# Four output tiles carried ahead of the last weights, and one even load of the first expert's w1

## The chip, the cores and the metric

The kernel runs on one core of a Trainium2 chip. The metric is the device time of one execution in microseconds (us).

## The reference, cut to what matters

```python
def _attn_ref(q, k, v):                       # (8, 8, 576, 64) each
    k_p = k.reshape(B, H, 72, 8, D).mean(axis=3)
    v_p = v.reshape(B, H, 72, 8, D).mean(axis=3)
    attn = softmax(scale * q @ k_p.T)         # 576 x 72 for each head
    return attn @ v_p
# x: the heads side by side, 4608 tokens x 512
def _moe_ref(x, phi, w1, w2):                 # 8 experts, 4 slots each, F = 1024
    logits = x @ phi                          # 4608 x 32
    d = softmax(logits, axis=0)               # over the tokens
    slot_input = (d.T @ x).reshape(8, 4, 512)
    for e in range(8):
        h = np.maximum(slot_input[e] @ w1[e], 0.0)
        slot_out[e] = h @ w2[e]
    c = softmax(logits, axis=1)               # over the 32 slots
    return c @ slot_out                       # 4608 x 512, float32
```

All inputs and the output are float32. w1 and w2 are 16 MB each in float32.

## The kernel before

**Loads.** All large loads are issued by GpSimd and cast to bfloat16 on the way. The order is written by hand: k, q and v of a pair of batches, then the next pair's, with w1 of the experts between them as soon as the second pair is in hand, then w2 behind the last v. `load_w1(0, 1, True)` (L105) sends the first expert's w1 in two column ranges. The first 2560 of the 4096 columns of a row go as rows 0 to 111, 112 to 119 and 120 to 127 (L110), the other 1536 columns of all rows follow in one transfer (L112). All other experts' w1 go in one transfer each time. The last part of w2 (expert 6 from its fourth block on, and expert 7) comes in two halves of 256 columns, each in four pieces (`PIECES`, L92; loads at L537). The very last piece of a half is one block, `J7`, of expert 7.

**Attention** takes the pairs of batches in turn: keys and values are pooled, scores, exponentials, and the products u (L338), from which also the logits come. It ends in `G`, the slot inputs, and `cT`, the transposed exponentials of the logits, in which each slot's weight for each token lies.

**First layer.** `hidden` (L559) and `turn_hidden` (L575) make `hT` for all experts. From here on the order of TensorE (PE), VectorE (DVE), ScalarE (ACT) and SyncE (SP) is the written one (`manual_schedule`, L550).

**Second layer.** `second_layer` (L583) adds into `so_ps`, one PSUM bank, with four groups of 32 partitions (g = fj % 4) that are added up later by the last product. The matmuls of the experts 0 to 3 run at once for all 512 columns; then come five `busy(512)` matmuls (L615), which compute nothing that is used, then experts 4 and 5, and the pieces of experts 6 and 7 as they land.

**Output.** A token tile n has 128 tokens; `GROUPS` (L57) joins 2, 2, 2, 4, 6, 8 and 12 tiles into areas of the output that are contiguous, `tokens(n)` picks a tile's columns of `cT`. `product` (L640) makes one tile in one of five PSUM banks, `put` scales its rows on ACT (engine 0) or DVE (engine 1), `store` (L636) issues the transfer on SP. Tiles 0 to 9 are made in two halves of columns, the first half while the second half's weights are loading; tiles 10 to 35 whole.

**Carrying.** In `begin(half)` (L662) the second layer's sum without `J7` is scaled to `so_a`. A carried tile gets `J7`'s share in another way: `zT` (L604 to L609) is `cT` times the hidden values of that block, so that zT times the piece of w2, plus tokens times `so_a`, is the finished tile before the last second-layer matmul has run. Before, tiles 0 and 1 are carried, tile 0 ahead of that last matmul and tile 1 behind it; `so`, the full sum, is scaled on DVE, and the tiles from 2 on use it. The stores of the first half are tile 0, 1, 2 and 3 one by one, then 4 and 5, 6 and 7, 8 and 9; those of the second half 0, 1, then 2 and 3, 4 and 5, 6 to 9; then three large ones of 1.5, 2 and 3 MB.

Of the kernel before, what the change touches and what calls it, by code (L numbers as in the profile page):

```python
# [8 lines left out]
FP = mybir.dt.float32  # L9
BF = mybir.dt.bfloat16  # L10
# [8 lines left out]
def kernel(  # L19
# [10 lines left out]
    nc = tc.nc  # L30
# [4 lines left out]
    DM = H * D  # L35
    E = moe_w1.shape[0]
    F = moe_w1.shape[2]
    NS = moe_phi.shape[1]
# [9 lines left out]
    DJ = DM // 128  # L48
    FJ = F // 128
# [23 lines left out]
    w1_sb = persist.tile([128, E, DJ, F], BF)  # L73
    cT = persist.tile([128, 2, B * S // 2], BF)
    hT = persist.tile([128, E, FJ, NS], BF)
# [14 lines left out]
    HC = DM // 2  # L90
    halves = [slice(0, HC), slice(HC, DM)]
# [4 lines left out]
    def load(src, pair):  # L96
        nonlocal loaded
        loaded += 1
        t = big[:, loaded % 4]
        nc.gpsimd.dma_start(out=t, in_=pair_of(src, pair))  # L100
        return t.rearrange("p (t d) -> p t d", d=D)

    UNEVEN = 2560

    def load_w1(e, n, uneven=False):  # L105
        dst = w1_sb[:, e:e + n].rearrange("p e j f -> p e (j f)")
        src = moe_w1[e:e + n].rearrange("e (p j) f -> p e (j f)", j=DJ)
        if uneven:
            for p0, p1 in ((0, 112), (112, 120), (120, 128)):
                nc.gpsimd.dma_start(out=dst[p0:p1, :, 0:UNEVEN], in_=src[p0:p1, :, 0:UNEVEN])  # L110
            dst, src = dst[:, :, UNEVEN:], src[:, :, UNEVEN:]
        nc.gpsimd.dma_start(out=dst, in_=src)  # L112

    w2_at = {}

# [55 lines left out]
    with tc.tile_pool(name="tmp", bufs=1) as tmp:  # L171
# [8 lines left out]
        for r in range(2):  # L180
            rows = slice(r * D, (r + 1) * D)
            nc.vector.tensor_copy(out=iphi[rows, :, r, 0:D],
                                  in_=ident[rows, rows].rearrange("p d -> p () d").to_broadcast([D, HQ, D]))
# [6 lines left out]
        for j in range(J):  # L190
            nc.tensor.matmul(out=phi_ps, lhsT=sel[:, j].rearrange("p r a j -> p (r a j)"), rhs=spread[:, j],  # L191
                             start=(j == 0), stop=(j == J - 1))
# [4 lines left out]
    hz = consts.tile([128, 128], BF)  # L197
# [13 lines left out]
    def after_k(p):  # L211
        if p + 1 < NP:
            q_sb[p + 1] = load(q, p + 1)
        if p == 1:
            load_w1(0, 1, True)

    def after_q(p):
        if p + 1 < NP:
            v_sb[p + 1] = load(v, p + 1)
        if p == 1:  # L220
            load_w1(1, 1)
        if p == 2:
            load_w1(2, 3)
            load_w1(5, 3)
# [35 lines left out]
    def prepare_kq(pair):  # L260

        means = kvpool.tile([128, NR, 2, D], BF, name="kmeans")
        yield from pool_stage(k_sb[pair], means, lambda: after_k(pair))
        kp[pair] = kvpool.tile([128, BH, SP], BF, name="kp", bufs=2)
        dst = kp[pair].rearrange("p n (r i) -> p r n i", r=NR)
        yield from turn_stage(means, lambda r0, r1, ps: nc.vector.tensor_copy(out=dst[:, r0:r1], in_=ps))
        for n, t0 in enumerate(range(0, NU, 6)):
            ps = ps_m.tile([128, 6, BH, NI], BF, name="q_ps", tag="m")
            for t in range(6):
                tt = 2 * (t0 + t)  # L270
                nc.tensor.transpose(out=ps[:, t].rearrange("p n i -> p (n i)"),  # L271
                                    in_=q_sb[pair][:, tt:tt + 2, :].rearrange("p t d -> p (t d)"), identity=ident)
            dst = qT[pair][:, :, t0:t0 + 6, :].rearrange("p n t i -> p t n i")
            if n % 3 == 1:
                nc.scalar.copy(out=dst, in_=ps)  # L275
            else:
                nc.vector.tensor_copy(out=dst, in_=ps)  # L277
            if n == NU // 6 - 1:
                after_q(pair)
            yield  # L280
# [133 lines left out]
    for g, (rows, base) in enumerate(GROUPS):  # L414
        cols = cT[:, :, base // 2:base // 2 + 64 * rows].rearrange("p r (i s) -> p s r i", s=rows // 2)
# [47 lines left out]
    def tokens(n):  # L463

        g, r = TILES[n]
        rows, base = GROUPS[g]
        step, c0 = rows // 2, base // 2 + r // 2
        return cT[:, r % 2, c0:c0 + 127 * step + 1:step]
# [63 lines left out]
    w2_half = {}  # L532
    for half, cols in enumerate(halves):
        for e, j0, j1 in PIECES:
# [3 lines left out]
                                in_=moe_w2[e].rearrange("(p j) d -> p j d", j=FJ)[:, j0:j1, cols])  # L538
# [12 lines left out]
    post = ctx.enter_context(tc.tile_pool(name="post", bufs=1))  # L551
    ps_o = ctx.enter_context(tc.tile_pool(name="ps_o", bufs=1, space=PSUM))
    ps_f = ctx.enter_context(tc.tile_pool(name="ps_f", bufs=5, space=PSUM))
# [26 lines left out]

    so_ps = ps_o.tile([128, DM], FP, name="so_ps")

    def second_layer(e, j0=0, j1=FJ, half=None):  # L583
        cols = slice(0, DM) if half is None else halves[half]
        for fj in range(j0, j1):
            g = fj % NG
            nc.tensor.matmul(out=so_ps[g * NS:(g + 1) * NS, cols], lhsT=hT[:, e, fj],  # L587
                             rhs=w2_at[e, fj] if half is None else w2_half[e, fj, half],
                             start=(e == 0 and fj < NG), stop=(e == E - 1 and fj >= NG), skip_group_check=True)

    hidden(0)
# [10 lines left out]
    J7 = FJ - 1  # L602
    P7 = (E - 1) % NG * NS
    nc.vector.tensor_scalar(out=hz[P7:P7 + NS], in0=h_sb[(E - 1) // NG][P7:P7 + NS, J7:F:FJ], scalar1=recC[P7:P7 + NS],  # L604
                            scalar2=None, op0=ALU.mult)
    z_ps = ps_f.tile([128, 2, 128], FP, name="z_ps", tag="f")
    nc.tensor.matmul(out=z_ps, lhsT=hz, rhs=cT[:, :, 0:128], start=True, stop=True)
    zT = post.tile([128, 2, 128], BF)
    nc.scalar.copy(out=zT, in_=z_ps)  # L609

    idle = ps_m.tile([128, 512], FP, name="idle_ps", tag="m")
# [3 lines left out]
    def busy(n):  # L615
        nc.tensor.matmul(out=idle[:, 0:n], lhsT=cTf[:, 0:128], rhs=cTf[:, 0:n], start=True, stop=True)

    def scaled(engine, dst, src, by):
        if engine == 0:
            nc.scalar.activation(out=dst, in_=src, func=AF.Copy, scale=by)  # L620
        else:
            nc.vector.tensor_scalar(out=dst, in0=src, scalar1=by, scalar2=None, op0=ALU.mult)  # L622

    so_a = post.tile([128, DM], BF)
    so = post.tile([128, DM], BF)
# [3 lines left out]
    n = 0  # L629
# [6 lines left out]
    def store(g, r0, r1, cols):  # L636
        home, dst = places[g]
        nc.sync.dma_start(out=dst[:, r0:r1, cols], in_=home[:, r0:r1, cols])

    def product(n, cols, carried=False):  # L640
        bank = ps_f.tile([128, DM], FP, name="f_ps", tag="f")
        ps = bank[:, 0:cols.stop - cols.start]
        if carried:
            half = halves.index(cols)
            nc.tensor.matmul(out=ps, lhsT=zT[:, n], rhs=w2_half[E - 1, J7, half], start=True, stop=False)
            nc.tensor.matmul(out=ps, lhsT=tokens(n), rhs=so_a[:, cols], start=False, stop=True)
        else:
            rhs, times = so[:, cols], 2 if cols == halves[0] and n >= 4 else 1
            nc.tensor.matmul(out=bank[:, 0:times * (cols.stop - cols.start)].rearrange("p (a c) -> p a c", a=times), lhsT=tokens(n),  # L649
                             rhs=rhs.rearrange("p c -> p () c").to_broadcast([128, times, cols.stop - cols.start]),  # L650
                             start=True, stop=True)
        return ps

    def rec(n):
        i, c = place[n]
        return recR[:, i, c:c + 1]

    def put(n, cols, engine, ps):
        g, r = TILES[n]
        scaled(engine, places[g][0][:, r, cols], ps, rec(n))  # L660

    def begin(half):  # L662

        cols = halves[half]
        scaled(0, so_a[:, cols], so_ps[:, cols], recC)
        f0 = product(0, cols, True)
        second_layer(E - 1, J7, FJ, half)
        f1 = product(1, cols, True)
        put(0, cols, 0, f0)
        store(0, 0, 1, cols)  # L670
        scaled(1, so[:, cols], so_ps[:, cols], recC)
        put(1, cols, 0, f1)
        store(0, 1, 2, cols)

    def tiles(n0, n1, half):

        cols = halves[half]
        for n in range(n0, n1):
            put(n, cols, 1 - n % 2, product(n, cols))
        g, r = TILES[n0]  # L680
        store(g, r, r + n1 - n0, cols)

    for e in range(4):
        second_layer(e)
    next(pieces)
    for _ in range(5):
        busy(512)
    for e in range(4, E - 2):
        second_layer(e)
    next(pieces)  # L690
    second_layer(E - 2, 0, CUT6)
    for (e, j0, j1), n in zip(PIECES[:-1], (256, 256, 192)):
        busy(n)
        second_layer(e, j0, j1, 0)
    begin(0)
    tiles(2, 3, 0)
    tiles(3, 4, 0)
    for n in (4, 6):
        tiles(n, n + 2, 0)
    for e, j0, j1 in PIECES[:2]:  # L700
# [1 line left out]
    tiles(8, 10, 0)  # L702
    for e, j0, j1 in PIECES[2:-1]:
        second_layer(e, j0, j1, 1)
    begin(1)
    tiles(2, 4, 1)
    tiles(4, 6, 1)
    tiles(6, 10, 1)
    for n in range(10, len(TILES)):
        g, r = TILES[n]  # L710
# [33 lines left out]
```

## Time and profile before

| | |
|---|---|
| median of 3 runs | 175.5 us (175.19 to 176.65) |
| the profiled execution | 175.59 us, of which its span is 173.8 |
| PE busy | 129.2 us (74%) |
| VectorE busy | 100.5 us (58%) |
| ScalarE busy | 88.3 us (51%) |
| GpSimd busy | 29.1 us (17%) |
| moved by DMA | 41.14 MB, mean 237 GB/s as written |
| granted TensorE clock, mean | 0.967 |

The span runs from the first instruction to the last. Loads are counted by what they write, bfloat16, so that they show about half of the bytes that are read. In the sections of the profile, L with a number is a line of the kernel; "out<-in" names the tiles that an instruction writes and reads; a name in brackets after an arrow is what ended an engine's idle time. PEld is the loading of weights into TensorE. In a table of windows, each row is a stretch of time with the busy time of each engine (and its number of instructions), the granted TensorE clock, the busy share of the 16 DMA engines and the GB/s that they wrote. A share over 1 means that transfers overlap on an engine.

### The profile page before, as it was taken

To read this page: it belongs to the slowest core of one execution; us is meant where nothing else is said; L and a number is where in the kernel's file an instruction comes from. 1 tells how busy PE (TensorE), PEld (TensorE's weight loads), DVE (VectorE), ACT (ScalarE), POOL (GpSimd) and SP (SyncE) were. 2 spreads that over 40 slices of the span, in tenths; PEclk is the share of its full clock that TensorE was granted. 3 is DMA by queue.
4 is the path that set the end of the run, shared out by engine and by line. 5 is a ranking of instruction groups with operands and counts; after the bars stand their busy time and mean duration, and the time that the engine had idled before them with its cause. 6 is when DMAs were issued, how large, how long until landed. Compare 5 with 4: busy or idle time off the path is not lost.

```text
span 173.8 us, 2873 instructions
## 1 busy us (share of the span) xinstructions
PE 129.2 (74%) x1106; PEld 69.9 (40%) x1106; DVE 100.5 (58%) x265; ACT 88.3 (51%) x168; POOL 29.1 (17%) x45
## 2 busy tenths in 40 slices
PE   0005788999899999999699998987999677798000
PEld 0002353565555656565354544453434233333000
DVE  6686354387869578797975688540651002599200
ACT  3201239886787738979205989374120004799100
POOL 7000111062101042007003441303310030000000
PEclk9999999999999999999999999999999999999655
DMA  5999999999999999999999999999999999999996
GB/s 196 247 214 221 210 221 214 216 218 210 213 195 226 215 213 223 214 211 216 219 215 219 213 217 215 217 217 219 215 213 219 203 193 195 305 329 431 445 407 272
DMA packets 10781, 41.14 MB, mean 237 GB/s; under 512 B 768, under 2 KB 6656, under 8 KB 7184
## 3 DMA queue, kind: packets, MB, share of 16 engines
q0 software_dynamic: 7440, 30.48, 86.7%
q1 hardware_dynamic: 3328, 10.49, 15.4%
q8 instruction: 8, 0.13, 0.3%
q14 instruction: 5, 0.04, 0.1%
HBM read 61.93 MB, written 9.44 MB: 411 GB/s over the span
## 4 chain that ended last, share of the span: by engine, by line
PE 31%; DMA 31%; ACT 14%; DVE 12%; issue 3%; POOL 1%; DVEq 0%; POOLq 0%; ACTq 0%
DMA qTa<-in_moe_w_dram 18%; PE pool_ps L239 10%; DMA phi_f<-in_moe_phi_dram 7%; ACT exa L318 7%; DMA xsa<-in_moe_w_dram 6%; PE sc L316 5%; DVE xsa L349 4%; PE u_ps L338 4%; PE q_ps L271 4%; DVE w_sb L622 4%; PE G_ps L373 2%; PE turn_ps L255 2%; ACT vmeans L245 2%; ACT vp L303 2%; ACT qTa L275 1%
## 5 line engine op out<-in xcount | busy, mean ns | idle before, releaser
L318 ACT ACTIVATE exa<-sc 72x576 bf16<-72x576 f32 x64 | 39.3, 653 | 4.6 <-PE sc L316 3.8
L349 DVE TENSOR_TENSOR xsa<-u_ps,rec 128x384 bf16<-128x384 f32 x69 | 37.8, 554 | 1.7
L338 PE MATMUL u_ps<-vp,exa 128*128 128x97 bf16 (+5 forms) x320 | 31.4, 229 | 3.6 <-DVE xsa L349 3.0
L338 PEld LDWEIGHTS <-exa 128*128 128x128 bf16 (+1 forms) x320 | 18.9, 100 | 15.7 <-DVE xsa L349 6.4
L316 PE MATMUL sc<-qTa,kp 64*72 64x288 bf16 x128 | 20.5, 303 | 1.7 <-ACT exa L318 1.2
L239 PE MATMUL pool_ps<-big,pmat 128*128 128x512 bf16 x64 | 18.0, 407 | 0.7 <-ACT qTa L275 0.6
L343 DVE RECIPROCAL rec<-u_ps 128x4 f32<-128x4 f32 x72 | 11.9, 175 | 10.8 <-PE u_ps L338 10.5
L275 ACT COPY qTa<-q_ps 128x768 bf16<-128x768 bf16 x8 | 6.3, 794 | 12.3 <-PE q_ps L271 12.3
L191 PE MATMUL phi_ps<-spread,sel 128*128 128x256 bf16 x4 | 1.3, 395 | 15.1 <-DVE spread L186 15.1
L271 PE MATMUL q_ps<-ident,big 128*128 128x128 bf16 x144 | 11.6, 219 | 0.8 <-DVE qTa L277 0.3
L649 PE MATMUL f_ps<-so,cT 128*128 128x512 bf16 (+1 forms) x42 | 10.7, 352 | 1.7 <-ACT w_sb L620 0.8
L316 PEld LDWEIGHTS <-kp 64*72 64x72 bf16 x128 | 7.7, 106 | 8.9 <-issue 3.5
L247 DVE TENSOR_REDUCE rsum<-rest_ps 128x64 f32<-128x512 f32 x8 | 5.5, 691 | 9.7 <-PE rest_ps L243 9.6
L622 DVE TENSOR_SCALAR w_sb<-f_ps,recR 128x512 f32<-128x512 f32 (+1 forms) x17 | 10.5, 682 | 0.6 <-PE f_ps L649 0.5
L277 DVE COPY qTa<-q_ps 128x768 bf16<-128x768 bf16 x16 | 8.7, 551 | 2.3 <-PE q_ps L271 2.2
L537 POOL DMA_DIRECT2D xsa<-in_moe_w_dram x8 | 5.9, 743 | 24.3 <-DMA qTa<-in_moe_w_dram 8.9
L620 ACT ACTIVATE w_sb<-f_ps,recR 128x512 f32<-128x512 f32 (+1 forms) x17 | 9.6, 638 | 0.7 <-PE f_ps L649 0.5
L271 PEld LDWEIGHTS <-big 128*128 128x128 bf16 x144 | 8.7, 97 | 3.0 <-issue 1.3
L373 PE MATMUL G_ps<-xsa,ee 128*128 128x512 bf16 x36 | 8.4, 379 | 1.2 <-ACT ee L368 1.2
L239 PEld LDWEIGHTS <-pmat 128*128 128x128 bf16 x64 | 6.0, 102 | 6.8 <-issue 2.4
L620 ACT ACTIVATE so_a<-so_ps,recC 128x256 bf16<-128x256 f32 x2 | 0.9, 473 | 14.8 <-PE so_ps L587 14.8
L245 ACT CAST vmeans<-pool_ps 128x1024 bf16<-128x1024 f32 x4 | 4.0, 1012 | 6.8 <-PE pool_ps L239 6.8
(110 smaller groups left out, 168.1 us busy)
## 6 DMA issues: line engine op xcount, KB each, us to landing
w_sb<-in_moe_w_dram POOLq DMA_DIRECT2D x2, 3072.0 KB, 38.7
big<-in_q_dram POOLq DMA_DIRECT2D x4, 1152.0 KB, 12.9
big<-in_v_dram POOLq DMA_DIRECT2D x4, 1152.0 KB, 16.7
big<-in_moe_w_dram POOLq DMA_DIRECT2D x1, 4096.0 KB, 35.3
big<-in_k_dram POOLq DMA_DIRECT2D x3, 1152.0 KB, 21.4
out_dram<-w_sb SPq DMA_DIRECT2D x1, 3072.0 KB, 10.8
qTa<-in_moe_w_dram POOLq DMA_DIRECT2D x1, 2048.0 KB, 32.0
out_dram<-w_sb SPq DMA_DIRECT2D x1, 2048.0 KB, 7.5
```

Of the source, the lines that this page charges most:

```text
L239: nc.tensor.matmul(out=ps, lhsT=pmat, rhs=src[:, t:full * POOL:POOL, :], start=(t == 0), stop=(t == POOL - 1))
L271: nc.tensor.transpose(out=ps[:, t].rearrange("p n i -> p (n i)"), in_=q_sb[pair][:, tt:tt + 2, :].rearrange("p t d -> p (t d)"), identity= ...
L277: nc.vector.tensor_copy(out=dst, in_=ps)
L316: nc.tensor.matmul(out=ps[:, r, 0:S // 2], lhsT=kp[pair][rows, n], rhs=qT[pair][rows, n].rearrange("p t i -> p (t i)"), start=True, stop=True)
L318: nc.scalar.activation(out=dst.rearrange("p r (i t) -> p r i t", t=NU), in_=ps[:, :, 0:S // 2].rearrange("p r (t i) -> p r i t", i=NI), fu ...
L338: nc.tensor.matmul(out=bank[rows, hh * UW:(hh + times) * UW].rearrange("p (a c) -> p a c", a=times), lhsT=ex[b][:, hh].rearrange("p r t -> ...
L343: nc.vector.reciprocal(out=rec, in_=ps[:, :, XW])
L349: nc.vector.tensor_tensor(out=dst, in0=ps[:, :, 0:XW], in1=rec.rearrange("p h -> p h ()").to_broadcast([128, HQ, XW]), op=ALU.mult)
L373: nc.tensor.matmul(out=ps, lhsT=ee[:, t].rearrange("p g s -> p (g s)"), rhs=x[:, t, :, 0:D], start=(t == 0), stop=(t == 8))
L620: nc.scalar.activation(out=dst, in_=src, func=AF.Copy, scale=by)
L622: nc.vector.tensor_scalar(out=dst, in0=src, scalar1=by, scalar2=None, op0=ALU.mult)
L649: nc.tensor.matmul(out=bank[:, 0:times * (cols.stop - cols.start)].rearrange("p (a c) -> p a c", a=times), lhsT=tokens(n), rhs=rhs.rearran ...
```

## The change

- w1 of the first expert goes in one transfer of 128 rows of 4096 columns.
- The matmuls of experts 0 to 3 in the second layer take their columns in steps of two (`by=2`: first the even columns, then the odd ones), in the weights read and in the PSUM bank written; three `busy(512)` follow instead of five.
- `zT` covers four tiles instead of two.
- `begin` carries the tiles 0 to 3 in both halves: four products with `zT`, four with `so_a`, then the last second-layer matmul. Tiles 0, 2 and 3 are put by ACT, tile 1 by DVE ahead of `so`. The stores keep their sizes and their order.

```diff
-    def load_w1(e, n, uneven=False):
-        dst = w1_sb[:, e:e + n].rearrange("p e j f -> p e (j f)")
-        src = moe_w1[e:e + n].rearrange("e (p j) f -> p e (j f)", j=DJ)
-        if uneven:
-            for p0, p1 in ((0, 112), (112, 120), (120, 128)):
-                nc.gpsimd.dma_start(out=dst[p0:p1, :, 0:UNEVEN], in_=src[p0:p1, :, 0:UNEVEN])
-            dst, src = dst[:, :, UNEVEN:], src[:, :, UNEVEN:]
-        nc.gpsimd.dma_start(out=dst, in_=src)
+    def load_w1(e, n):
+        nc.gpsimd.dma_start(out=w1_sb[:, e:e + n].rearrange("p e j f -> p e (j f)"),
+                            in_=moe_w1[e:e + n].rearrange("e (p j) f -> p e (j f)", j=DJ))
...
-    def second_layer(e, j0=0, j1=FJ, half=None):
+    def second_layer(e, j0=0, j1=FJ, half=None, by=1):
...
-            nc.tensor.matmul(out=so_ps[g * NS:(g + 1) * NS, cols], lhsT=hT[:, e, fj],
-                             rhs=w2_at[e, fj] if half is None else w2_half[e, fj, half],
+            rhs = w2_at[e, fj] if half is None else w2_half[e, fj, half]
+            nc.tensor.matmul(out=so_ps[g * NS:(g + 1) * NS, cols].rearrange("p (c s) -> p s c", s=by), lhsT=hT[:, e, fj],
+                             rhs=rhs.rearrange("p (c s) -> p s c", s=by),
...
-    z_ps = ps_f.tile([128, 2, 128], FP, name="z_ps", tag="f")
-    nc.tensor.matmul(out=z_ps, lhsT=hz, rhs=cT[:, :, 0:128], start=True, stop=True)
-    zT = post.tile([128, 2, 128], BF)
+    CARRY = 4
+    z_ps = ps_f.tile([128, 2, 128 * CARRY // 2], FP, name="z_ps", tag="f")
+    nc.tensor.matmul(out=z_ps, lhsT=hz, rhs=cT[:, :, 0:128 * CARRY // 2], start=True, stop=True)
+    zT = post.tile([128, 2, 128 * CARRY // 2], BF)
...
-    def begin(half):
+    def begin(half, stores):
         cols = halves[half]
         scaled(0, so_a[:, cols], so_ps[:, cols], recC)
-        f0 = product(0, cols, True)
+        f = []
+        for n in range(CARRY):
+            f.append(ps_f.tile([128, DM], FP, name="f_ps", tag="f")[:, 0:HC])
+            nc.tensor.matmul(out=f[n], lhsT=zT[:, n % 2, n // 2 * 128:n // 2 * 128 + 128], rhs=w2_half[E - 1, J7, half],
+                             start=True, stop=False)
+        for n in range(CARRY):
+            nc.tensor.matmul(out=f[n], lhsT=tokens(n), rhs=so_a[:, cols], start=False, stop=True)
         second_layer(E - 1, J7, FJ, half)
-        f1 = product(1, cols, True)
-        put(0, cols, 0, f0)
-        store(0, 0, 1, cols)
+        put(0, cols, 0, f[0])
+        put(1, cols, 1, f[1])
+        put(2, cols, 0, f[2])
         scaled(1, so[:, cols], so_ps[:, cols], recC)
-        put(1, cols, 0, f1)
-        store(0, 1, 2, cols)
+        put(3, cols, 0, f[3])
+        for g, r0, r1 in stores:
+            store(g, r0, r1, cols)
...
     for e in range(4):
-        second_layer(e)
+        second_layer(e, by=2)
     next(pieces)
-    for _ in range(5):
+    for _ in range(3):
         busy(512)
...
-    begin(0)
-    tiles(2, 3, 0)
-    tiles(3, 4, 0)
+    begin(0, ((0, 0, 1), (0, 1, 2), (1, 0, 1), (1, 1, 2)))
...
-    begin(1)
-    tiles(2, 4, 1)
+    begin(1, ((0, 0, 1), (0, 1, 2), (1, 0, 2)))
     tiles(4, 6, 1)
```

More of the change, by code (lines that the diff above doesn't have):

```diff
@@ L101, in load @@
         return t.rearrange("p (t d) -> p t d", d=D)
-    UNEVEN = 2560
-    def load_w1(e, n, uneven=False):
-        dst = w1_sb[:, e:e + n].rearrange("p e j f -> p e (j f)")
-        src = moe_w1[e:e + n].rearrange("e (p j) f -> p e (j f)", j=DJ)
-        if uneven:
-            for p0, p1 in ((0, 112), (112, 120), (120, 128)):
-                nc.gpsimd.dma_start(out=dst[p0:p1, :, 0:UNEVEN], in_=src[p0:p1, :, 0:UNEVEN])
-            dst, src = dst[:, :, UNEVEN:], src[:, :, UNEVEN:]
-        nc.gpsimd.dma_start(out=dst, in_=src)
+    def load_w1(e, n):
+        nc.gpsimd.dma_start(out=w1_sb[:, e:e + n].rearrange("p e j f -> p e (j f)"),
+                            in_=moe_w1[e:e + n].rearrange("e (p j) f -> p e (j f)", j=DJ))
     w2_at = {}
@@ L214, in after_k @@
         if p == 1:
-            load_w1(0, 1, True)
+            load_w1(0, 1)
     def after_q(p):
@@ L638, in store, with product @@
         nc.sync.dma_start(out=dst[:, r0:r1, cols], in_=home[:, r0:r1, cols])
-    def product(n, cols, carried=False):
+    def product(n, cols):
         bank = ps_f.tile([128, DM], FP, name="f_ps", tag="f")
[L642 to L652, printed above, removed]
+        rhs, times = so[:, cols], 2 if cols == halves[0] and n >= CARRY else 1
+        nc.tensor.matmul(out=bank[:, 0:times * (cols.stop - cols.start)].rearrange("p (a c) -> p a c", a=times), lhsT=tokens(n),
+                         rhs=rhs.rearrange("p c -> p () c").to_broadcast([128, times, cols.stop - cols.start]),
+                         start=True, stop=True)
+        return bank[:, 0:cols.stop - cols.start]
     def rec(n):
```

## The prediction

> **What bounds the kernel now.** I read the page first: the slices, then the queues.
>
> ```profile
> DMA  5999999999999999999999999999999999999996
> ...
> q0 software_dynamic: 7440, 30.48, 86.7%
> ```
>
> The 16 DMA engines are busy in every slice but the first and the last. GpSimd's queue (q0, the loads, cast on the way) fills 86.7% of the span of 173.8; most of the rest is stores. Each load ends on its slowest engine, since a landing counts when all 16 are through. The second view is the chain of waits, in its last third.
>
> ```profile
> 106.94 32.03 DMA qTa<-in_moe_w_dram
> 139.52 9.70 DMA xsa<-in_moe_w_dram
> 149.26 0.31 PE so_ps L587 x3
> 149.59 0.48 ACT so_a L620
> 150.12 0.27 PE f_ps L646
> 150.39 0.23 PE so_ps L587
> 150.71 0.49 DVE so L622
> ```
>
> From 107 to 149.3 us the chain is loads alone: compute waits for the last pieces of w2. Then a short compute chain makes output tiles, and the stores finish. How full the DMA engines are after that is read from windows of time:
>
> ```profile
> core 0: us, PE busy (x) PEld busy (x) DVE busy (x) ACT busy (x) POOL busy (x), PEclk, DMA share, GB/s
> 149.40:150.00 0.60, 0.43 (x4) 0.11 (x2) 0.00 (x0) 0.59 (x2) 0.00 (x0) 1.00 0.51 172
> ...
> 152.90:153.50 0.60, 0.60 (x4) 0.31 (x3) 0.47 (x2) 0.60 (x2) 0.00 (x0) 1.00 0.34 113
> 153.50:156.40 2.90, 2.70 (x11) 1.01 (x9) 2.90 (x5) 2.90 (x6) 0.00 (x0) 1.00 1.05 354
> 156.40:172.50 16.10, 4.13 (x14) 1.50 (x12) 5.60 (x9) 4.67 (x8) 0.00 (x0) 0.69 1.00 423
> ```
>
> ```profile
> 155.49 0.34 SPq L638 DMA_DIRECT2D out_dram<-w_sb  x1
> ```
>
> There are two short holes, 0.6 x 0.49 = 0.29 us and 0.6 x 0.66 = 0.40 us of idle engine time. From 153.5 on there is none. The last row is from the timeline: the first of the three large stores (1.5 MB, tiles 10 to 15) is issued at 155.49, and its data runs from about 156.4 with no break to 172.5. So the end is 18.3 us behind that issue if the store comes just in time, or is set by the sum of DMA work if it queues. Either way time is won only by making the loads end earlier, by making tiles 10 to 15 earlier, or by filling the holes.
>
> **The change part by part.** *The first expert's w1.* It was sent as rows 0 to 111, 112 to 119 and 120 to 127 of 2560 columns and then the other 1536 columns of all rows; it becomes one transfer of 128 rows of 4096. The bytes are the same. Three GpSimd issues of about 0.52 us go, in a stretch where the landing takes 15 to 21 us from the issue, so they hide nothing and cost nothing. What the split costs the engines shows where it is moved:
>
> ```profile
> L110 POOL DMA_DIRECT2D w_sb<-in_moe_w_dram x3: 502/519/559, 35.7 to 36.8; - x3
> ...
> DMA to landing us min/median/max: 15.1/15.7/21.5
> ```
>
> ```profile
> 45.00:47.00 2.00, 1.72 (x21) 1.04 (x18) 1.94 (x8) 2.00 (x5) 0.31 (x1) 1.00 0.98 205
> 47.00:49.00 2.00, 1.78 (x16) 1.01 (x15) 1.54 (x6) 1.92 (x5) 0.00 (x0) 1.00 1.13 207
> 49.00:51.00 2.00, 2.00 (x18) 1.19 (x19) 1.32 (x4) 2.00 (x5) 0.00 (x0) 1.00 0.94 179
> 51.00:53.00 2.00, 1.78 (x19) 0.94 (x18) 1.66 (x6) 1.25 (x3) 0.53 (x1) 1.00 1.14 232
> 53.00:55.00 2.00, 1.85 (x26) 1.22 (x24) 2.00 (x6) 1.45 (x4) 0.00 (x0) 1.00 1.01 212
> ```
>
> ```profile
> 65.00:71.00 6.00, 5.84 (x65) 3.68 (x64) 4.81 (x15) 5.34 (x12) 1.33 (x2) 1.00 1.03 217
> ```
>
> Issued at 35.7 and up, landing 15 us later, the split w1 passes at 46 to 53. The five windows move (205 + 207 + 179 + 232 + 212) / 5 = 207 GB/s, the even loads of 65 to 71 move 217: 10 us x (1 - 207/217) = 0.46 us lost, with the engines shown as busy (1.13, 1.14) and moving less. The even transfer returns this on average. For the last engine it is another matter. One row of 2560 f32 is 10 KB, and an engine moves 423/16 = 26.4 GB/s, so a row is 0.39 us. If the two small transfers lie on the same half of the engines, that half carries 9 such rows and the other 7, against 8 when even. A slowest engine that carried 9 wins 0.46 + 0.39 = 0.85 us, one that carried 7 wins 0.07. The views do not say which it is. I take 0.5, the mean gain with little added, and keep 0.07 and 0.85. This gain passes to all later loads, which follow without a break, and so to the landing at 149.26.
>
> *The carried tiles, first half.* Before, one carried tile stood ahead of the last w2 matmul and one behind it; tiles 2 and 3 waited for `so`. Now all four are multiplied first. The rows of before:
>
> ```profile
> 145.73 0.27 PE L646 MATMUL f_ps<-so_a,cT 128*128 128x256 bf16 x1 [0.24 <-ACT so_a L620]
> 145.93 0.28 PE L587 MATMUL so_ps<-xsa,hT 128*32 128x256 bf16 x1
> 146.04 1.01 ACT L620 ACTIVATE exa<-f_ps,recR 128x256 f32<-128x256 f32 x2 [0.36 <-PE f_ps L646]
> 146.32 0.48 DVE L622 TENSOR_SCALAR so<-so_ps,recC 128x256 bf16<-128x256 f32 x1 [5.49 <-PE so_ps L587]
> 146.54 2.66 SPq L638 DMA_DIRECT2D out_dram<-exa  x5
> ```
>
> A matmul of 256 columns follows the last by 0.11 us (0.215 for 512, halved; the eight groups of L587 below give 0.215). Tile 0 is ready as before. Tile 1 goes to VectorE at about 146.2 instead of to ScalarE at 146.55, `so` slips behind it to about 146.7 (+0.37), and ScalarE does tiles 2 and 3 at about 146.5 and 146.9, where before they waited for `so`, tile 2 till 147.2. The stores of tiles 1, 2, 3 start 0.2 to 0.4 us earlier. What is queued behind `so`, the products of tiles 4 to 9, is 0.1 to 0.3 us later on PE but not in its stores, since SP issues them one behind the other at 2.66/5 = 0.53 us each. None of this is on the path to the landing at 149.26. It has a price there: the stores share the engines with the last loads. 128 KB over 16 engines is 0.31 us each. Nothing if they only use idle engines, 0.31 if one more store gets ahead of the slowest engine's last load; I take 0.1.
>
> *Second half.* Here the chain is the end's. `so_a` at 149.59 and the first product at 150.12 stay; products 1 to 3 follow at 0.11 us and the w2 matmul at about 150.65 (before 150.39).
>
> ```profile
> 151.56 0.88 DVE L622 TENSOR_SCALAR exa<-f_ps,recR 128x256 f32<-128x256 f32 x2 [0.36 <-PE f_ps L649]
> 152.35 9.65 DVE L622 TENSOR_SCALAR w_sb<-f_ps,recR 128x256 f32<-128x256 f32 x15
> ```
>
> VectorE now does tile 1 at 150.55 and `so` at 151.04 (+0.33); product 4 ends 0.37 us behind `so` as before, and tiles 4, 6, 8 follow from 151.9 at 0.40 us each (two in 0.88 with 0.48 the last) to 153.1, where before, counted on from 151.56 at the same pace, tiles 2, 4, 6, 8 ended at 153.2. Tile 1 takes the place of tile 2 on VectorE and fills a wait of before; ScalarE has tiles 0, 2 and 3 instead of 0, 1 and 3. The stores up to tile 9 gain some 0.3 us, which goes into the second hole and not to the end. Tile 11 then waits for its product, as before, at about 153.3, since its bank comes free with tile 6 or 7. I take -0.05 for tiles 10 to 15; the bounds are +0.33, if `so`'s lateness goes through, and -0.15, where tile 11 follows tile 8 at once.
>
> *Strided matmuls.* The 32 matmuls of the first four experts read and write every second column, and five idle matmuls become three.
>
> ```profile
> 129.91 1.91 PE L587 MATMUL so_ps<-big,hT 128*32 128x512 bf16 x32
> 132.90 4.56 PE L616 MATMUL idle_ps<-cT 128*128 128x512 f32 x10
> 139.01 1.05 PE L587 MATMUL so_ps<-qTa,hT 128*32 128x512 bf16 x16 [1.55 <-DMA qTa<-in_moe_w_dram]
> 116.13 0.39 PE L436 MATMUL R_ps<-cT,onehot 128*10 128x512 bf16 x1
> L436 PE MATMUL R_ps<-cT,onehot x10: 271/554/854, 116.1 to 132.6; 128*10 128x512 bf16 x8, 128*10 128x256 bf16 x2
> ```
>
> Two idle ones less is 4 of the 10 passes at 0.43: -1.7 us. Reading with a step of 2 costs little (0.39 at 116.13, against 0.38 unstrided); the slowest strided row takes 0.854. So eight groups of four cost between +0 and 8 x 0.5 = +4 us. The nearest row says 0.39 for the read; a write with a step has no row, so I take +1.7. The cover is PE's wait of 1.55 us at 139.01; over that, the waits for pieces up to 144.9 take most, and only the first half's stores would be late. Cost: 0. The wider z product and its cast lie in the same stretch.
>
> By the Trainium skill, "SBUF — State Buffer" (Door 1: The DMA port swizzle, its note on cachelines), PSUM has 8-byte lines and a non-contiguous PSUM access slows matmuls considerably; that speaks against these 32, and no run here shows it yet. If it makes them three times as long, that estimate is +3.5 us, less 1.7 for the idle ones, and the sum stays the same.
>
> The sum, on the profiled execution of 175.59: -0.5 + 0.1 - 0.05 + 0 = **175.14**. The median of the runs shown, 175.5, is 0.09 below that execution, so about 175.05; I say 175.1.
>
> **Rivals.** *The last loads give nothing.* The slowest engine carried 7 rows (0.07) and the earlier stores take that back: 175.5. For it: no view shows the engine. Against: 0.46 lost on average. *Holes close.* 0.85 from w1, and 0.3 + 0.4 us of holes filled by earlier stores, if the 1.5 MB store queues and its issue does not bind: 175.5 - 1.5 = 174.0. Against: no slack is seen between its issue and its data. *Stores overtake loads (slower).* The fourth and the fifth store (128 and 256 KB, 0.31 + 0.62 us an engine) get ahead of the slowest engine's last pieces: +0.93 - 0.5 = 175.9. It decides from more than 0.5 us, about 210 KB, ahead. Against: the fifth store starts at most 0.25 us earlier. *The clock falls (slower).* If the stride is free, PE's wait at 139 becomes 1.55 + 1.7 = 3.2 us.
>
> ```profile
> 160.75 0.38 PE L649 MATMUL f_ps<-so,cT 128*128 128x512 bf16 x1 [0.20 <-ACT w_sb L620]
> 162.00:163.00 1.00, 0.00 (x0) 0.00 (x0) 0.00 (x0) 0.00 (x0) 0.00 (x0) 0.72 1.00 426
> ```
>
> After the last matmul ended at 161.13 the granted clock fell to a half at about 162.4 (0.72 over that window), while 1.55 us idle at 137.5 left it at 1.00. At half clock five matmuls in a row at 150 cost about 0.6 us and products at 0.43 us for tiles 10 to 15, against 0.33 for two evicting engines (9.65 us for two tiles at 0.40 and 13 at 0.68 on VectorE), another 0.6: 175.1 + 1.2 = 176.3. It needs the clock to stay down for 11 us of work. The Trainium skill, "TensorE: Matmul & The Clock Gate" (Part 1), puts the idle window at about 3.4 us, free-running; the two rows agree with a free-running window.
>
> **How the numbers follow.** Forecast 0.50 (own range 174.6 to 175.6), no gain 0.20, holes close 0.14, stores overtake 0.10, clock 0.06. The range goes from the holes' case to the clock's, 173.9 to 176.4. What a measurement of this kernel can tell from no change is about 1%, 1.75 us; only the far ends of the holes' case and of the slower cases reach that: 0.06 and 0.06.
>
> **What would show it.** Windows at 45 to 55 at 215 GB/s or more, without the 179; the wait for the last xsa piece ending at 148.7 to 149.1; VectorE's first put at about 1 us behind `so_a`; the 1.5 MB store issued at 154.9 to 155.2; PE's wait before the qTa matmuls between 0 and 3 us. The forecast is wrong if the last piece lands no earlier, or if it does and the 1.5 MB store is issued no earlier.

## The result, and the profile after

The change takes 174.72 us, the median of 22 runs (174.6 to 176.56), against 175.52 for the kernel before in the same comparison (22 runs, 174.95 to 177.38). The ratio is 0.9949, interval [0.9925, 0.9972]: half a per cent faster, inside the 1% that the prediction called no change. The profiled execution of the change is not one of the typical ones. It took 175.47 us, because the granted TensorE clock fell to a half for 3.41 us in it. "Unfallen" below means a run whose mean granted clock was at least 0.967, "fallen" one below that. 16 of the 22 runs are unfallen, and all of these lie at 174.60 to 175.26, most at 174.6 to 174.73, with a median of 174.69.

The windows of time in which the first w1 passes, in the change:

```profile
45.00:47.00 2.00, 1.71 (x24) 1.07 (x22) 1.96 (x7) 2.00 (x5) 0.53 (x1) 1.00 0.98 206
47.00:49.00 2.00, 1.78 (x16) 0.96 (x15) 1.63 (x5) 1.92 (x5) 0.00 (x0) 1.00 1.08 226
49.00:51.00 2.00, 2.00 (x19) 1.18 (x19) 1.41 (x4) 2.00 (x5) 0.00 (x0) 1.00 0.94 197
51.00:53.00 2.00, 1.96 (x21) 1.00 (x17) 1.47 (x5) 1.25 (x2) 0.47 (x1) 1.00 1.04 217
53.00:55.00 2.00, 1.77 (x25) 1.33 (x26) 2.00 (x8) 1.45 (x5) 0.06 (x1) 1.00 1.05 221
```

The mean is 213 GB/s where it was 207, and the 179 has become 197. The timeline of the change shows the strided matmuls and what pays for them:

```profile
130.32 3.62 PE L582 MATMUL so_ps<-big,hT 128*32 128x512 bf16 x32
135.01 2.84 PE L612 MATMUL idle_ps<-cT 128*128 128x512 f32 x6
138.19 1.05 PE L582 MATMUL so_ps<-qTa,hT 128*32 128x512 bf16 x16 [0.34 <-DMA qTa<-in_moe_w_dram]
```

The 32 matmuls went from 1.91 to 3.62 us (+1.71), the idle passes from 4.56 to 2.84 (-1.72). The qTa matmuls start at 138.19, not at 139.01, since the load they wait for landed 0.8 us earlier. PE itself came 0.4 us later in this execution (its 32 matmuls start at 130.32, not at 129.91), so its wait shrank by 1.2 us, to 0.34.

The chain of waits of this execution does not show the gain arriving at the end, and the windows of 3.41 us around the fall show why (the last three columns are the granted clock, the DMA share and GB/s):

```profile
143.50 0.94 PE idle_ps L612 x2
144.78 0.97 PE f_ps L659 x4
...
149.59 0.48 ACT so_a L616
...
151.03 0.50 DVE so L618
```

```profile
139.15:142.56 3.41, 2.25 (x20) 1.29 (x16) 0.40 (x2) 0.00 (x0) 0.89 (x2) 0.99 1.42 193
142.56:145.97 3.41, 3.23 (x18) 1.73 (x17) 0.00 (x0) 0.47 (x1) 0.00 (x0) 0.51 1.45 196
145.97:149.38 3.41, 2.76 (x23) 1.04 (x22) 2.26 (x5) 2.27 (x6) 0.00 (x0) 1.00 1.15 244
```

The clock is at a half for one window. `so_a` of the second half starts at 149.59 as before, although the last pieces came earlier: PE, not a load, stands ahead of it now (idle matmuls and carried products at half speed are in the chain). The first large store of this execution went out at 155.43, where before it was 155.49. The same edits without the stride, traced with the clock up (the experiment called unstrided below, one execution of 174.73 us), show the gain:

```profile
148.54 0.29 PE L582 MATMUL so_ps<-xsa,hT 128*32 128x256 bf16 x3
148.87 0.47 ACT L616 ACTIVATE so_a<-so_ps,recC 128x256 bf16<-128x256 f32 x1
149.81 0.48 DVE L618 TENSOR_SCALAR exa<-f_ps,recR 128x256 f32<-128x256 f32 x1 [1.05 <-PE f_ps L662]
```

```profile
154.71 0.34 SPq L634 DMA_DIRECT2D out_dram<-w_sb  x1
```

The last w2 matmuls start 0.72 us earlier than the 149.26 of before, and the 1.5 MB store is issued 0.78 us earlier.

### The profile page after: what moved, and what is told of

It is laid out like the page before. It is cut to its first block, busy times and chain, and to the rows that moved or that the text cites. A ratio compares the mean times of both kernels' runs of the same rounds, so it can differ in the third digit from the quotient of the medians.

```text
span 173.7 us, 2867 instructions
## 1 busy us (share of the span) xinstructions
PE 130.5 (75%) x1106; PEld 70.3 (40%) x1106; DVE 100.9 (58%) x265; ACT 88.1 (51%) x168; POOL 27.5 (16%) x42
## 4 chain that ended last, share of the span: by engine, by line
PE 36%; DMA 20%; ACT 16%; DVE 13%; issue 7%; POOL 2%; DVEq 0%; ACTq 0%; POOLq 0%
DMA xsa<-in_moe_w_dram 13%; PE pool_ps L232 10%; DMA phi_f<-in_moe_phi_dram 7%; ACT exa L311 7%; DVE xsa L342 6%; PE u_ps L331 5%; PE sc L309 5%; PE q_ps L264 4%; PE G_ps L366 2%; PE f_ps L639 2%; DVE w_sb L618 2%; PE turn_ps L248 2%; ACT vmeans L238 2%; ACT vp L296 2%; ACT w_sb L616 1%
## 5 line engine op out<-in xcount | busy, mean ns | idle before, releaser
L232 PE MATMUL pool_ps<-big,pmat 128*128 128x512 bf16 x64 | 18.2, 410 | 0.7 <-ACT qTa L268 0.6
L639 PE MATMUL f_ps<-so,cT 128*128 128x512 bf16 (+1 forms) x38 | 10.1, 361 | 2.0 <-DVE so L618 1.3
L530 POOL DMA_DIRECT2D xsa<-in_moe_w_dram x8 | 5.9, 743 | 23.1 <-DMA qTa<-in_moe_w_dram 8.9
```

The lines of the kernel that those rows point to most:

```text
L232: nc.tensor.matmul(out=ps, lhsT=pmat, rhs=src[:, t:full * POOL:POOL, :], start=(t == 0), stop=(t == POOL - 1))
```

## The experiments

### Each half of the change alone

The even transfer alone: the kernel before with one call changed.

```diff
-            load_w1(0, 1, True)
+            load_w1(0, 1)
```

> The kernel before with the first expert's w1 in one even transfer, nothing else changed. Theory A (the split held up the slowest DMA engine, and with it the last w2 pieces and the end): 174.7 to 175.1 us, with the last xsa piece landing 0.5 to 0.85 us earlier than before. Rival B (the gain of the change comes from the four carried tiles): 175.5, no change. Rival C (the landing comes earlier, but the first half's products hold up the second half's start, so nothing arrives at the end): last piece earlier by 0.5 or more, time 175.3 to 175.5.

Measured: 174.78 (12 runs, 174.72 to 176.44), ratio 0.9966 [0.9927, 1.0006]. The eight unfallen runs have 174.72 to 174.94, against 175.06 to 176.0 for the 20 unfallen runs of the kernel before beside it (medians 174.75 and 175.31). The interval of the ratio, over fallen and unfallen runs together, reaches 1; among the unfallen runs none of the eight is as slow as the fastest of the 20. One call gives nearly all of what the change gives. The traced execution is a fallen one (176.44), so it does not show the landing of the last piece, but its qTa load, ahead of the fall, is early as in the change: the matmuls that wait for it start at 138.19.

The carried tiles alone: the new `begin` and the wider z product, w1 still in four transfers, no stride.

```diff
+    CARRY = 4
-    z_ps = ps_f.tile([128, 2, 128], FP, name="z_ps", tag="f")
+    z_ps = ps_f.tile([128, 2, 128 * CARRY // 2], FP, name="z_ps", tag="f")
...
-        second_layer(e, by=2)
+        second_layer(e)
-    for _ in range(3):
+    for _ in range(5):
```

> The kernel before with four carried tiles in both halves, w1 still split, no strided matmuls, five idle matmuls. Theory A: 175.4 to 175.6, and the second hole of the DMA engines (near 153 us) shorter with a new one ahead of the 1.5 MB store. Rival B: 174.7 to 175.0. Rival C: a part of the gain here too, since the half ahead of the second start is shorter: 175.1 to 175.3.

Measured: 175.46 (12 runs, 174.91 to 177.81), ratio 0.9995 [0.9955, 1.0035]. Only five runs were unfallen, 174.91 to 175.10; a gain of 0.35 over the 175.31 seemed to show there. The last four experiments below put that right.

### The stride alone, and the change without it

Both edits concern `second_layer(e, by=2)` and the count of idle matmuls, 3 with the stride and 5 without.

> The changed kernel with the experts 0 to 3 unstrided and five idle matmuls again (even w1 and four carried tiles stay). If the stride edit costs nothing (theory A): 174.7, as the change, with the same spread of runs. If the longer stretch of real work on TensorE keeps its clock (rival D): here more runs show the granted clock falling at 142 to 146 us, and they stand near 175.4; the median is 174.7 to 175.4.

Measured: 174.72 (12 runs, 174.58 to 176.2), ratio 0.9958 [0.9927, 0.9989], the same as the change; 3 of the 12 are fallen, where 6 of the change's 22 were, so rival D is not seen either.

> The kernel before with only the strided matmuls of experts 0 to 3 and three idle matmuls. Theory A: 175.5, no change; the 32 matmuls take about 3.6 us instead of 1.9 (as in the changed kernel), the three idle ones 2.8 instead of 4.6, and TensorE waits before the qTa matmuls as before. Rival D (it decides on the clock): another share of runs with a fallen clock, so 0.2 us or more either way.

Measured: 175.41 (12 runs, 174.97 to 178.41), ratio 1.0003 [0.9963, 1.0042]. The seven unfallen runs have a median of 175.18, against 175.31 for the kernel before beside it. That is small beside the spread of these runs, so the stride with the two missing idle matmuls shows no clear cost and no clear gain.

### What of the split costs time

Two even transfers of 2560 and 1536 columns keep the smaller pieces per row but not the 112, 8 and 8 rows:

```diff
-            for p0, p1 in ((0, 112), (112, 120), (120, 128)):
+            for p0, p1 in ((0, 128),):
```

> The kernel before with the first expert's w1 still in two column ranges, 2560 and 1536, but each in one transfer of all 128 rows. Theory A1 (the 8-row transfers are what holds the engines up): as the even transfer, 174.8 us in runs whose clock did not fall. Rival A2 (the shorter packets and the extra transfers cost it): about half of the gain is lost, 175.0 to 175.2.

Measured: 174.98 (12 runs, 174.78 to 176.51), ratio 0.9955 [0.9919, 0.9991]; the ten unfallen runs have a median of 174.91, against 175.14 for the 19 unfallen runs of the kernel before beside it and 174.75 for the single transfer, which ran in another comparison. By these medians the even rows bring 0.23 us and the single transfer another 0.16. That is between the theory and the rival, and the two are not parted: the uneven rows cost something, and the second transfer with its shorter rows may cost nearly as much.

The opposite, the second expert's w1 split in the same way:

```diff
-            load_w1(1, 1)
+            load_w1(1, 1, True)
```

> The kernel before with the second expert's w1 split into 112, 8 and 8 rows as well. Theory A1 (each split moves rows onto the same engines): the loss doubles, 175.7 to 175.9 in undisturbed runs against 175.25 of before, and the 2 us windows where the second w1 passes (about 56 to 61) fall to 200 GB/s or less. Rival (the second split falls on the other engines and evens the first out): the last landing stays or comes earlier, 175.2.

Measured: 175.84 (12 runs, 175.58 to 177.42), ratio 1.0013 [0.9975, 1.0051]; the nine unfallen runs have a median of 175.82, the 19 of the kernel before beside it 175.14. The windows in which the second expert's w1 passes, in the kernel before and then in this one:

```profile
57.00:59.00 2.00, 1.98 (x25) 1.42 (x25) 1.05 (x4) 2.00 (x4) 0.00 (x0) 1.00 1.05 218
59.00:61.00 2.00, 2.00 (x17) 1.13 (x15) 1.15 (x3) 0.99 (x2) 0.00 (x0) 1.00 1.07 225
```

```profile
57.00:59.00 2.00, 1.98 (x25) 1.43 (x25) 1.05 (x4) 2.00 (x4) 0.00 (x0) 1.00 1.03 206
59.00:61.00 2.00, 2.00 (x17) 1.12 (x15) 1.15 (x3) 0.99 (x2) 0.00 (x0) 1.00 1.01 187
```

Where the second split passes, a dip appears that was not there: 206 and 187 GB/s, with the engines as busy as 1.01 to 1.03. By the medians the second split costs about 0.7 us more. But the 19 runs beside it mix early and late ones (the last experiments show the two groups), and this kernel has no early one: all nine unfallen runs have 175.58 or more. Its traced execution is no later than the traced kernel before, with a span of 173.8 in both.

### The clock held by more idle matmuls

These two edits are called the filler below.

```diff
     next(pieces)
+    busy(256)
     second_layer(E - 2, 0, CUT6)
-    for (e, j0, j1), n in zip(PIECES[:-1], (256, 256, 192)):
+    for (e, j0, j1), n in zip(PIECES[:-1], (384, 256, 192)):
```

> The changed kernel with two more idle matmuls in TensorE's waits at 139 to 142 us: busy(256) ahead of expert 6's first blocks, and 384 instead of 256 columns behind them. Theory D (the clock falls when TensorE is busy for less than about 2.28 of a 3.41 us window there): no run has a fallen clock at 142, all stand at 174.6 to 174.8, none at 175.3 to 175.5. Rival (the fall has another cause): a quarter of the runs still at 175.3 or more.

Measured: 174.69 (12 runs, 174.63 to 174.86), ratio 0.9921 [0.989, 0.9951]. None of the 12 runs has a fallen clock, where 6 of the change's 22 and 3 of the unstrided's 12 had. The windows of this kernel:

```profile
138.80:142.20 3.40, 3.00 (x26) 1.33 (x18) 0.40 (x2) 0.00 (x0) 1.24 (x2) 1.00 1.40 193
142.20:145.60 3.40, 2.89 (x20) 1.71 (x20) 0.27 (x1) 0.85 (x3) 0.00 (x0) 1.00 1.45 195
```

PE is busy 3.00 of 3.40 us in about the stretch (138.8 to 142.2) in which the fallen execution had 2.25 of 3.41 (139.15 to 142.56). The lowest times did not move (174.63 against 174.60), so no cost of the filler shows.

### The large store in two

In the trace of the change a hole of 0.2 us lies ahead of the 1.5 MB store's data. Tiles 10 to 12 were stored by themselves:

```diff
+        if g == 4 and r == 2:
+            store(g, 0, 3, slice(0, DM))
...
-            store(g, 0, GROUPS[g][0], slice(0, DM))
+            store(g, 3 if g == 4 else 0, GROUPS[g][0], slice(0, DM))
```

> The changed kernel with the 1.5 MB store issued in two parts, tiles 10 to 12 and 13 to 15. Theory E (the issue of that store binds the end: a hole of about 0.17 us of the DMA engines lies ahead of its data): 0.1 to 0.2 us faster than the change in undisturbed runs, 174.5. Rival (the sum of DMA work binds): no difference, 174.7, or slower by the additional store's share.

Measured: 175.02 (12 runs, 174.88 to 178.19), ratio 0.996 [0.9925, 0.9994]: 0.3 slower than the change, unfallen against unfallen. The windows around the hole, with the store whole (the filled change) and then in two:

```profile
155.80:156.10 0.30, 0.30 (x2) 0.12 (x1) 0.30 (x2) 0.30 (x2) 0.00 (x0) 1.00 1.54 655
156.10:156.40 0.30, 0.30 (x2) 0.12 (x1) 0.30 (x1) 0.30 (x2) 0.00 (x0) 1.00 0.39 164
```

```profile
155.80:156.10 0.30, 0.30 (x2) 0.12 (x1) 0.30 (x2) 0.30 (x2) 0.00 (x0) 1.00 1.07 430
156.10:156.40 0.30, 0.30 (x2) 0.12 (x1) 0.30 (x1) 0.30 (x2) 0.00 (x0) 1.00 0.97 389
```

The hole is gone, and the span is 173.2 instead of 172.9. The second part of the store is issued at 154.63, as the whole one was in the filled change (154.62), and yet the end came later. What the stretch behind the data spends in the second case was not found; it stays open.

### Both halves again, with the filler

The four corners got the same filler and ran together: neither half of the change (before_filled), the even w1 (even_filled), the carried tiles (carry_filled) and both (both_filled). None has the stride.

> The kernel before with one idle matmul more (256 wide) ahead of the second expert-layer piece and one idle matmul widened from 256 to 384, nothing else. Theory: PE is now busy for more than 2.3 us of any 3.41 us around 142 us, so the granted clock never falls; the runs whose clock was .957 to .965 vanish and all of them lie where the unfallen ones of the kernel before lay: median 175.15 to 175.3, none above 175.8. Rival (the filler itself delays the path, since PE is late in this stretch): a floor 0.2 us higher, 175.4 to 175.5. Rival (the fall has nothing to do with PE's idle time): a third of the runs stay above 175.8.

Measured: 175.5 (12 runs, 174.82 to 177.18), ratio 0.9987 [0.9944, 1.0029]. Three runs fell all the same, so the expectation that none would is wrong.

> The kernel before with the first w1 in one even transfer, and the same filler. With the clock held, the even transfer alone: 174.75 (0.45 us below before_filled). Rival (even w1 was worth only the 0.1 of the packets, the rest was the clock): 175.1.

Measured: 174.8 (12 runs, 174.71 to 176.66), ratio 0.9941 [0.9903, 0.998]. The nine unfallen runs have 174.71 to 174.86; three fell.

> The kernel before with four tiles carried on both sides (w1 still uneven, matmuls unstrided) and the same filler. With the clock held: 174.95 (0.25 below before_filled), since its unfallen runs lay at 174.91 to 175.10. Rival (carrying gives nothing, the 0.25 was a choice of runs): 175.2. Rival (carrying's gain is in its being less hurt by a fallen clock): 175.2 as well, and then no different from before_filled.

Measured: 175.33 (12 runs, 174.87 to 176.13), ratio 0.9958 [0.9922, 0.9994]. The eleven unfallen runs come in two groups: five of 174.87 to 175.01 and six of 175.31 to 175.66. The forecast, 174.95, fits the first group alone.

> Even w1 and four tiles carried, unstrided, the same filler. If both parts save time by themselves the sum is 0.45 + 0.25 = 0.7 below before_filled: 174.45 to 174.6. If the two overlap (both only shorten the wait for the same last loads) it is 174.65 to 174.75, as the strided version with the filler had 174.69.

Measured: 174.7 (11 runs, 174.57 to 174.8), ratio 0.9914 [0.988, 0.9947]. None fell.

The two groups are the find of this set. The unfallen runs of the first corner split likewise, three of 174.82 to 175.11 and six of 175.36 to 175.67; both kernels with the even w1 have one group. In the runs of the kernel before without the filler the times are spread from 174.82 to 176.0 with no clear gap. The profiled runs happened to catch one of each group among the uneven kernels. First the filled kernel before (174.92 us), then the filled kernel with carried tiles (175.39 us), rows of the timeline and of the window in which the first w1 passes:

```profile
148.59 0.29 PE L587 MATMUL so_ps<-xsa,hT 128*32 128x256 bf16 x3 [0.20 <-DMA xsa<-in_moe_w_dram]
148.93 0.47 ACT L620 ACTIVATE so_a<-so_ps,recC 128x256 bf16<-128x256 f32 x1
```

```profile
45.00:55.00 10.00, 9.28 (x91) 5.43 (x89) 8.00 (x24) 8.37 (x16) 1.06 (x2) 1.00 1.04 213
```

```profile
149.17 0.29 PE L589 MATMUL so_ps<-xsa,hT 128*32 128x256 bf16 x3
149.52 0.47 ACT L623 ACTIVATE so_a<-so_ps,recC 128x256 bf16<-128x256 f32 x1
```

```profile
45.00:55.00 10.00, 9.27 (x98) 5.54 (x96) 8.47 (x25) 8.62 (x17) 1.05 (x2) 1.00 1.04 209
```

Both have the same split w1. In one execution it passes at 213 GB/s, and the last w2 matmuls start at 148.59; in the other at 209, and they start at 149.17. The profiled kernel before, 175.59 us with its matmuls at 149.26, is of the late group.

The other traces agree. GpSimd waits for the qTa load ahead of its next issue (L537 before, L530 in the change), and the end of this wait parts the traces. In the three executions with one split w1 where it ends at 139.45 to 139.52 (before, stride_only, carry_filled), the ten us from 45 to 55 move 207, 204 and 209 GB/s. In the two others with one split w1 (before_filled, carry_only) they move 213 and 212, in those with an even one 212 to 215, and in all of these the wait ends at 138.68 to 138.85. two_experts_split fits too: its first split passes at 212, its second in the dip shown above, and the wait ends at 139.52. So in these traces the lateness goes with a slow passing of a split w1. The mean over the 16 engines loses only about 10 us x (1 - 207/213) = 0.3 us there, while the later load comes about 0.7 us late. That fits some engines falling behind by more than the mean, which is the theory, but no view shows a single engine, so it is argued and not shown.

The two filled kernels with the even w1:

```profile
148.52 0.29 PE L587 MATMUL so_ps<-xsa,hT 128*32 128x256 bf16 x3 [0.16 <-DMA xsa<-in_moe_w_dram]
148.85 0.47 ACT L620 ACTIVATE so_a<-so_ps,recC 128x256 bf16<-128x256 f32 x1
```

```profile
148.82 0.47 ACT L616 ACTIVATE so_a<-so_ps,recC 128x256 bf16<-128x256 f32 x1
```

So the uneven w1 does not make each run later by the same amount: in more than half of the unfallen runs of the two filled kernels (12 of 20) the time is that of the late group, whose traced last piece is about 0.6 us late, and in the rest it costs about 0.1. What decides between the two from run to run is not settled.

## Why the prediction was right or wrong

**The total.** Forecast 175.1 in a range of 173.9 to 176.4; measured 174.72, which is no change by the 1% that it set. The forecast's own range, 174.6 to 175.6, held it, but low in it. The sum was made against an execution of 175.59 and gave -0.45; typical runs of the change lie near 174.7, which is -0.9 from there. The term of the even w1 was too small, and the two of the carried tiles together had the wrong sign. With the sizes that the runs show against that execution, -0.7 and -0.1, the sum gives 174.79.

**The even w1, -0.5.** Right in place and sign, and the bounds, 0.07 and 0.85, were the better part of the step. The prediction said that a slowest engine with 9 rows wins 0.85 and one with 7 wins 0.07, and that no view says which. The runs fit both kinds of case in one kernel: even_filled (174.79, median of the unfallen) lies 0.13 below the early group of before_filled (median 174.92) and 0.72 below its late group (175.51). The profiled execution stood in the late group, so against its own time the term is -0.7. Taking "the mean with little added" as one fixed number was the slip; a fixed share of rows for the slowest engine would have made one group, not two. How many rows the slowest engine carried, no run shows. The signs came out in part. The windows, forecast at 215 or more without the 179, have a mean of 213, with one of 197. The wait for the last piece, forecast to end at 148.7 to 149.1, ended sooner: the matmuls behind it start at 148.41 to 148.54 in the unfallen traces with an even single transfer.

**Carried tiles, +0.1 and -0.05.** Taken together as a loss of 0.05, measured as a gain of 0.1 at most: with even w1 and the filler 174.79 became 174.70; in the late group of the uneven kernels 175.51 became 175.40, in the early group 174.92 became 174.95. The 1.5 MB store agrees: it is issued at 154.74 in even_filled and at 154.66 in both_filled. The price of +0.1 for earlier stores beside the last loads was not seen: the last w2 matmuls start at 148.52 without the carried tiles and at 148.54 with them (even_filled, unstrided). What I read into carry_only at first, a gain of 0.35, was most likely the group: its five unfallen runs, 174.91 to 175.10, lie where the early ones of carry_filled lie.

**Second half.** The order came as worked out. VectorE's first put stands 149.81 - 148.87 = 0.94 us behind `so_a`, where the prediction had about 1. The store was issued at 154.71, just ahead of the 154.9 to 155.2 forecast, by the part of the w1 term that was missing. That the end follows this issue held too: 0.78 us earlier there, and the unstrided's profiled span is 173.0 against 173.8. In all 13 traces with this store whole the span ends 18.2 to 18.4 us behind its issue, as the 18.3 of the prediction had it.

**Strided matmuls, 0.** The idle ones came as worked out, -1.7 expected and -1.72 measured. The +1.7 for the strided ones, measured at +1.71, was luck: it was picked from a range of 0 to +4, with no row for a strided write. PE's wait at qTa, forecast between 0 and 3 us, is 0.34 in the change. It is not a fixed cover: it was 1.55 before, 1.94 in stride_only and nothing in the unstrided, where PE came to these matmuls later, at 138.69, and the end was as early. The rule of the Trainium skill that was weighed here ("SBUF — State Buffer", Door 1: a non-contiguous PSUM access slows matmuls considerably) agrees with this row, at 1.9 times the time and not the three times of the estimate; read and write were strided together, so the runs do not part the two.

**The rivals.** *Last loads give nothing* is refuted by even_only. *Holes close* happened in part and brought little. In the traced filled change the two holes, 0.29 and 0.40 us before, are down to about 0.07 and 0.15, but a third of about 0.18 stands ahead of the large store's data; with this third hole gone the time went up. *Stores overtake loads* is not seen, by the equal 148.5 above. *The clock falls* is real, but not as I had it. I put it at PE's wait ahead of the qTa matmuls and priced it at 1.2 us. In the traced execution it came at about 142.5 us, for one window of 3.41 us. 6 of the change's 22 runs are fallen, and five of these have that execution's clock of 0.959 and 175.35 to 175.48 us: 0.7 to 0.8 us more. It was also no product of the change. Of the 104 runs of the kernel before in the three comparisons 47 had a clock below 0.967, and the highest of these reach 178. Among unfallen runs alone the change (174.69) lies 0.45 to 0.62 below the kernel before (175.14 to 175.31 in the three comparisons). So a part of the 0.8 us between the two medians probably comes from falls of the kernel before; whether the change lowers their chance, 6 of 22 against 47 of 104 do not settle.

**What the filler settles.** Each stretch of 3.41 us just ahead of a fall near 142 us that was traced has PE busy for at most 2.29 us (change 2.25, even_only 2.24, carry_only 2.29, stride_only 1.92). The filled change and both_filled, with more work in that stretch, had no fall in 23 runs, where the same kernels without filler had 9 in 34. That is hardly chance, though the runs come from several comparisons, so for these kernels the filler very likely holds the clock. In before_filled and even_filled it did not suffice, 3 of 12 fallen in each, nor in carry_filled (1 of 12), and their fallen runs were not traced. The version to keep is the change with the filler, or the same without the stride: ratios 0.9921 [0.989, 0.9951] and 0.9914 [0.988, 0.9947].

## What to carry to other kernels

Where a stream of loads sets the end, look for transfers of a few rows, which may not spread evenly over the DMA engines: here the lag from one split w1 was still there in the loads 85 to 100 us later, and a single call was worth more than a reordering of the compute behind it. Before a term is priced from one profiled execution, find out whether that execution is typical; here the kernel before, with the filler, has two groups of runs 0.5 us apart and, besides, falls of the clock, and a gain of 0.35 us read from five runs was most likely nothing but the draw of the group. When an engine is left half idle on purpose, ask what its clock does with that, and test it with a few idle matmuls.

## What the hardware showed that I had not expected

The granted clock fell although PE was never idle for long. In even_only's trace it stays down for two windows (columns as above):

```profile
138.83:142.24 3.41, 2.24 (x23) 1.17 (x16) 0.39 (x2) 0.00 (x0) 1.21 (x2) 0.99 1.40 192
142.24:145.65 3.41, 3.17 (x13) 1.11 (x13) 0.00 (x0) 0.47 (x1) 0.00 (x0) 0.50 1.45 195
145.65:149.07 3.42, 3.31 (x14) 1.21 (x17) 1.89 (x4) 1.90 (x5) 0.00 (x0) 0.51 1.18 228
```

PE was busy for 2.24 of 3.41 us, and the next window ran at half clock. In the profiled kernel before the clock falls at about 162.4; five such lengths earlier, 162.4 - 5 x 3.41 = 145.4, a window ends in which 2.29 us were busy, and the clock stayed up:

```profile
142.00:145.40 3.40, 2.29 (x17) 1.27 (x17) 0.00 (x0) 0.19 (x1) 0.00 (x0) 1.00 1.45 195
```

Later in even_only's trace, in a window that the same steps of 3.41 us give, PE was busy for 2.23 us, and the clock stayed up through the next:

```profile
159.31:162.72 3.41, 2.23 (x8) 0.75 (x6) 3.41 (x6) 2.57 (x5) 0.00 (x0) 1.00 0.96 404
162.72:166.13 3.41, 0.00 (x0) 0.00 (x0) 0.09 (x1) 0.00 (x0) 0.00 (x0) 0.99 1.18 500
```

So busy time alone gives no sharp limit in these traces: of the windows with 2.23 to 2.29 us some are followed by a fall and some are not, and what decides there is open. Where such a window begins differs from trace to trace (falls at 141.39, 142.24 and 142.56), which is one reason why a stretch this thin may fall in some runs and not in others. The Trainium skill, "TensorE: Matmul & The Clock Gate" (Part 1), tells of a free-running window of about 3.4 us and warns of idle gaps as long as the window. The length agrees with the 3.41 us here. The warning about gaps is too narrow here: PE was without work for only a third of the window, spread over several short waits, and the clock fell.

The other surprise is the two groups: one 112, 8 and 8 row split, 100 us ahead of the end, makes the last load about 0.6 us late in some executions of a kernel and nearly leaves it in place in others.
